# A recurrent cross-attention block feeding an act_gcu block: another order for the first pair of batches, and three moves in the later pairs

## The chip, the cores and the metric

The kernel runs on one core of one Trainium2 chip. A core has TensorE (PE, matmuls; its weight loads are shown as PEld), VectorE (DVE), ScalarE (ACT), GpSimd (POOL), and SyncE (SP), which here only issues DMAs. Each engine works through its own queue in order and waits on semaphores. The metric is the device time of one execution in microseconds (us). Before the change the median of three runs is 735.45 us (733.81 to 736.73).

## The reference

Eight batches, eight heads, 512 tokens and 32 states of width 64 each, in float32; the two weights of the second block come as float64.

```python
scores = scale * x @ state^T;  a = softmax(scores)      # 512 x 32 per head
xread  = a @ state
scores2 = scale * state @ x^T; a2 = softmax(scores2)    # 32 x 512 per head
sread  = a2 @ x
x = concat([xread, sread], axis=2) as (B*544, 512)      # 4352 tokens
h = x @ w_in                                            # 512 -> 2048
g = h * cos(h)
out = g @ w_out                                         # 2048 -> 512
```

## The kernel before, in words

**Layers.** For each batch b the 512 token rows go through 16 tiles f of 128 columns of d_ff ("tile" below is one such f). The attention matrix is not multiplied by the states first: `products` (line 452) multiplies the states with a 512-column part nt of w_in, `products_kept` (457) copies the result into `sw`, and `hidden` (483) multiplies `sw` by the attention matrix `aT` into a PSUM bank h. Then g = h cos(h) in four steps: `gate` (560, ACT, rounds h), `gate2` (567, DVE, the difference), `gate3` (570, ACT, sine), `gate4` (574, DVE, the product into `g_all`). `gate4` is the last reader of h, so a later tile that uses the same bank waits for it. After the eight batches the 256 state rows go through a layer of 16 tiles of their own, the states' layer, and through `state_products`.

**Pairs.** Two batches form a pair. The product with w_out is done for a pair by a Strassen-Winograd scheme: 7 products (class `Product`, 719) of 7 stages each (`ORDER`, 664). A stage (`multiply`, 761) is 8 matmuls of 256 columns in the trace. `follow` (778) is what the other engines do behind a stage: behind stage 1 ACT copies the lower half of the bank and its upper half away, and stage 2 adds into that lower half, so it can only start behind the copies. The sums of columns and rows that the scheme needs are `outer_sum` (1066, DVE or POOL) and `Product.sums` (738, POOL); `halves`, `sw_sums` and `seven_part` (502, 516, 532) do `hidden` for batches 2 to 7 in the same manner, with 7 part products for two tiles. `gate` to `gate4` then work on a pair of tiles, 1024 columns at a time.

**The first pair** (batches 0 and 1, steps 0 to 31) also has to load the float64 weights and make float32 of them. `convert` (213) takes one load of 1 MB in five instructions: ACT "1" and "2" (the magnitude, the low word), DVE "b" (shift left by 3) and "c" (take over the sign, exclusive or), POOL "d" (add the low part). There are 4 half loads (512 columns) and 14 whole ones (1024 columns). For the 14 the shift "b" writes to the two side banks of PSUM (`h_pairs[1]`), and "c" reads it there.
The order of the first pair is not written out. `first_pair_tasks` (1125) lists tasks with an engine, a cost, what they read and write, and a due time in steps; `link` (1524) finds their dependences; `first_pair` (1560) is a planner that puts them on the five queues one by one. It takes the engine that can start soonest; among the tasks of that engine that can start within `NEAR` of the soonest it takes the one due first. A task marked `shares` is a DVE instruction that the planner counts as sharing its memory port with POOL: before the change neither starts while the other's (`lock`) lasts. Where PE would idle long before its first product, it gets filling matmuls (`warm`, 951).

**The later pairs** (from step 32 on) have an order written out by hand: `later_pair` (1638) issues one step. In an even step ACT does `gate` and DVE `gate2`, in an odd step ACT does `gate3` and DVE `gate4`; `go(n)` issues the attention's pieces of list n that `plan` (973) put at this step; `stages` (1099) issues the step's stages of `Product`, one or two. At the end of a step the main loop issues `outer_sum` for that step. In the states' layer `hidden(coming)` issues 8 matmuls for the tile two steps ahead.

Of the kernel before, what the change touches and what calls it, by code (L numbers as in the profile page):

```python
# [11 lines left out]
I32 = mybir.dt.int32  # L12
# [10 lines left out]
def kernel(  # L23
# [189 lines left out]
    def convert(i, p):  # L213
# [8 lines left out]
        shifted = bits if i < 4 else h_pairs[1].bitcast(I32)  # L222
# [6 lines left out]
        elif p == "b":  # L229
            nc.vector.tensor_scalar(shifted, bits, 3, None,  # L230
                                    op0=ALU.logical_shift_left)
        elif p == "c":
            nc.vector.scalar_tensor_tensor(out=bits, in0=raw[:, :, :, 1],  # L233
                                           scalar=-2 ** 31, in1=shifted,
                                           op0=ALU.bitwise_and,
                                           op1=ALU.bitwise_xor)
        else:
            nc.gpsimd.tensor_tensor(bits, bits, e, op=ALU.add)  # L238
# [10 lines left out]
    class Attention:  # L249
# [207 lines left out]
        def products_kept(self, nt, bank=None, c0=0, c1=WC, copy=None,  # L457
                          js=(0, 1)):
            to = at if bank is None else side_banks
            if (self.b, nt) not in sw_of:  # L460
# [258 lines left out]
    class Product:  # L719
# [4 lines left out]
        def __init__(self, name, pr, row):  # L724
# [6 lines left out]
            self.t1 = self.t2 = self.t3 = None  # L731
# [242 lines left out]
    def plan(b):  # L974
        pe, x_act, y_act, x_dve, y_dve, z_act = [
            {s: [] for s in range(NF)} for _ in range(6)]

        def prod(s, b, nt, *bank):
            pe[s].append((b, "products", nt) + bank)
            x_act[s].append((b, "products_kept", nt) + bank)  # L980
# [36 lines left out]
        return pe, x_act, y_act, x_dve, y_dve, z_act  # L1017
# [107 lines left out]
    def first_pair_tasks():  # L1125
# [35 lines left out]
        def conversion(i, due):  # L1161
# [4 lines left out]
            x, narrow = (w, True) if i < 4 else ("sd00 sd01 sd10 sd11", False)  # L1166
            b_cost = n * .0007 + .03 if narrow else dve(n)
            for p, engine, cost, r, wr, sh in (
                    ("1", "act", act(n) + .05, raw, w, False),
                    ("2", "act", act(n) + .05, raw, e, False),  # L1170
                    ("b", "dve", b_cost, w, x, narrow),
                    ("c", "dve", dve(n), raw + " " + x, w, narrow),
# [4 lines left out]
        def attention(b, k):  # L1177
# [30 lines left out]
            m2 = k + 6 if b == 0 else k + 1.0  # L1208
            if b == 0:
                for j in range(2):  # L1210
                    add("dve", .62, lambda j=j: a.sums1((j,)), f"z{z}{j}",
                        f"m1{j}", k + 5)
                add("dve", .46, a.inverse1, "m10 m11", "m10 m11", k + 5,
                    True)
# [9 lines left out]
            if b == 0:  # L1224
                add("act", .2, a.exp2_bias, "m20 m21", "m20 m21", m2)
                for j in range(2):
                    add("act", .72, lambda j=j: a.exp2((j,)),
                        f"at{j} m2{j}", f"xT{2 + j} i2{j} T", m2)
                add("dve", .3, a.inverse2, "i20 i21", "i20 i21", m2 + 2,
                    True)  # L1230
            else:
                add("act", 5.0, a.exps, "at0 at1 m20 m21",
                    f"z{z}0 z{z}1 xT2 xT3 i20 i21 m20 m21", m2)
                for j in range(2):
# [3 lines left out]
                    "m10 m11 i20 i21", k + 7, True)  # L1238
# [54 lines left out]
        def tile_(t, k):  # L1293
# [11 lines left out]
                k + 1.5)  # L1305
# [97 lines left out]
        def p5_tasks(k):  # L1403
# [3 lines left out]
            for i, (r, w) in enumerate(((lo, q1), (hi + " " + q1, q1),  # L1407
                                        (lo + " " + hi, q3)), 1):
                add("pool", 2 * pool(512), lambda i=i: pd.sums(i), r, w,
# [3 lines left out]
            for i in range(5):  # L1413
# [12 lines left out]
                elif i == 2:  # L1426
                    add("dve", .36, follow, "acc0 sums1", "sums2", at_)
                    add("pool", 2 * pool(512), lambda: pd.sums(4),
# [6 lines left out]
        def p3_sums(k):  # L1435
            pd = products_[1]
            add("pool", 2 * pool(512), lambda: pd.sums(1),
# [17 lines left out]
        for step, what in (  # L1455
                (1, lambda: attention_late(0, 7.5)),
                (3, lambda: products(0, 1, 2)),
                (3, lambda: add("pe", .4, lambda: states(1, side_banks[0]),
                                "held0", "sd00 sd01", 7.0)),
                (3, lambda: add("act", .53,  # L1460
                                lambda: states_kept(1, side_banks[0]),
                                "sd00 sd01", "stT1", 10.0)),
                (5, lambda: attention(1, 3)),
                (7, lambda: products(0, 2, 8.5)),
                (11, lambda: products(0, 3, 19.5)),
                (13, lambda: products(1, 0, 21.5)),
                (13, lambda: attention_late(1, 10.0)),
                (13, lambda: inner(0, a11, 5, temps[0], names(TEMPS), 13.0)),
                (15, lambda: sends(2, a22, 8, 17)),
                (15, lambda: sums_of(SQ, A21, A22, add_, 16, "pool")),  # L1470
                (16, lambda: products(1, 1, 16.5)),
                (16, lambda: inner(3, matrix(SQ), SQ, temps[1], E, 16.5)),
                (17, lambda: sums_of(A22, SQ, A11, sub_, 26.5, "pool")),
                (17, lambda: attention(2, 23.5)),
                (18, lambda: sums_of(A21, A11, A21, sub_, 20.0, "dve")),
                (20, lambda: products(1, 2, 14.5)),
                (20, lambda: inner(5, matrix(A21), A21, temps[0],
                                   names(TEMPS), 25.5)),
                (20, lambda: sends(1, a12, 6, 22)),
                (21, lambda: inner(4, matrix(A22), A22, temps[1], E, 28.5)),  # L1480
                (23, lambda: sums_of(SQ, A12, A22, sub_, 32.0, "dve")),
                (24, lambda: inner(6, matrix(SQ), SQ, temps[0], names(TEMPS),
                                   25)),
                (24, lambda: products(1, 3, 27.5)),
# [269 lines left out]
```

## Time and profile before

| what | value |
|---|---|
| three runs | 733.81, 735.45, 736.73 us |
| the profiled execution | 736.73 us, of which the span from first to last instruction is 734.9 us |
| PE busy | 709.1 us (96%) |
| DVE, ACT, POOL busy | 501.4 (68%), 347.0 (47%), 535.5 (73%) |
| 0 to 40 us: PE, DVE, ACT, POOL busy | 32.67, 26.74, 24.03, 15.17 us |
| 40 to 102 us, of 62 | 57.32, 58.55, 56.85, 40.81 us |
| 102 to 158 us, of 56 | 55.49, 45.83, 34.43, 45.31 us |
| 158 to 616 us, of 458 | 450.88, 317.73, 212.86, 365.44 us |
| 616 to 734.9 us, of 118.9 | 112.69, 52.59, 18.84, 68.82 us |

The page gives averages over stages with different limits, so the table cuts the span: the first pair lasts to about 158 us, the later pairs to about 616 us, and the rest is the states' layer and the end. In the trace a float32 matmul appears as two; a tile of the first pair (`hidden`, line 489) is 4 matmuls of 512 columns, 1.72 us at full clock, start to start. A row "x4" of the timeline merges four instructions; PE's records run over into the next by some 0.2 us, so lengths are best read from start to start.

### The profile page before, as it was taken

To read this page: it belongs to the slowest core of one execution; us is meant where nothing else is said; L and a number is where in the kernel's file an instruction comes from. 1 tells how busy PE (TensorE), PEld (TensorE's weight loads), DVE (VectorE), ACT (ScalarE), POOL (GpSimd) and SP (SyncE) were. 2 spreads that over 40 slices of the span, in tenths; PEclk is the share of its full clock that TensorE was granted. 3 is DMA by queue.
4 is the path that set the end of the run, shared out by engine and by line. 5 is a ranking of instruction groups with operands and counts; after the bars stand their busy time and mean duration, and the time that the engine had idled before them with its cause. 6 is when DMAs were issued, how large, how long until landed. Compare 5 with 4: busy or idle time off the path is not lost.

```text
span 734.9 us, 10754 instructions
## 1 busy us (share of the span) xinstructions
PE 709.1 (96%) x3628; PEld 519.4 (71%) x3628; DVE 501.4 (68%) x703; ACT 347.0 (47%) x586; POOL 535.5 (73%) x524
## 2 busy tenths in 40 slices
PE   8798899999999999999999999999999999999997
PEld 4343344467778788786778787877778788888886
DVE  4889979868767567849756687768665367355551
ACT  4699975644544455443634373444634533211110
POOL 1557599557998896579989665879989665799600
PEclk9799999999999999999999999999999999999999
DMA  9787598736346954682248635763235465346652
GB/s 296 255 229 246 177 280 264 174 103 141 86 136 140 217 141 127 133 197 79 81 96 162 159 87 116 157 145 87 72 75 129 112 211 133 103 157 206 162 146 46
DMA packets 204021, 111.33 MB, mean 151 GB/s; under 512 B 149888, under 2 KB 166784, under 8 KB 203968
## 3 DMA queue, kind: packets, MB, share of 16 engines
q1 hardware_dynamic: 202880, 110.14, 57.6%
q8 instruction: 29, 0.48, 0.3%
q10 hardware_dynamic: 960, 0.39, 0.2%
q14 instruction: 24, 0.20, 0.1%
q0 software_dynamic: 128, 0.13, 0.1%
HBM read 87.03 MB, written 23.59 MB: 151 GB/s over the span
## 4 chain that ended last, share of the span: by engine, by line
PE 64%; POOL 21%; DVE 7%; issue 3%; DMA 3%; ACT 2%; SPq 0%; ACTq 0%; DVEq 0%; POOLq 0%
PE o L774 29%; POOL g_all L716 16%; PE h L544 13%; PE h L489 10%; POOL swS_all L522 3%; PE at L313 3%; PE o L641 3%; PE at L879 2%; PE at L418 2%; POOL sw_all L522 2%; DMA g_all<-in_moe_w_in_dram 1%; DMA g_all<-blocks_kept 1%; DVE h L230 1%; PE o L879 1%; DVE w_in L233 1%
## 5 line engine op out<-in xcount | busy, mean ns | idle before, releaser
L716 POOL TENSOR_TENSOR g_all<-g_all 128x512 f32<-128x512 f32 x252 | 333.1, 1352 | 63.9 <-DVE g_all L716 40.8
L774 PE MATMUL o<-g_all 128*128 128x256 f32 x1456 | 344.1, 381 | 2.9 <-POOL g_all L716 2.4
L774 PEld LDWEIGHTS o<-g_all 128*128 128x128 f32 x1456 | 273.6, 190 | 50.8 <-issue 5.0
L565 ACT ACTIVATE q_all<-h 128x1024 int32<-128x1024 f32 (+1 forms) x88 | 73.3, 833 | 86.8 <-PE h L544 37.8
L568 DVE TENSOR_TENSOR q_all<-q_all,h 128x1024 f32<-128x1024 int32 (+1 forms) x88 | 85.2, 969 | 40.2 <-ACT q_all L565 40.0
L585 DVE TENSOR_TENSOR g_all<-h,q_all 128x1024 f32<-128x1024 f32 (+1 forms) x88 | 85.6, 973 | 23.6 <-ACT q_all L571 22.7
L571 ACT ACTIVATE q_all<-q_all,halfpi 128x1024 f32<-128x1024 f32 (+1 forms) x88 | 84.0, 956 | 33.6 <-DVE q_all L568 33.3
L552 DVE TENSOR_TENSOR h<-h,sums_all 128x256 f32<-128x256 f32 x96 | 41.2, 429 | 76.6 <-PE h L544 59.4
L489 PE MATMUL h<-aT_all,sw_all 128*128 128x512 f32 x128 | 63.7, 627 | 4.8 <-DVE g_all L585 4.3
L544 PE MATMUL h<-aS_all,swS_all 128*128 128x256 f32 x192 | 60.3, 396 | 3.1 <-ACT sums_all L530 2.3
L544 PE MATMUL h<-aT_all,sw_all 128*128 128x256 f32 x192 | 59.6, 392 | 3.8 <-DVE g_all L585 3.4
L716 DVE TENSOR_TENSOR g_all<-g_all 128x1024 f32<-128x1024 f32 x42 | 59.9, 1440 | 0.1
L544 PE MATMUL h<-aS_all,sw_all 128*128 128x256 f32 x192 | 58.0, 384 | 0.1
L544 PEld LDWEIGHTS h<-aS_all,swS_all 128*128 128x128 f32 x192 | 33.8, 189 | 27.8 <-issue 12.1
L522 POOL TENSOR_TENSOR swS_all<-sw_all 128x128 f32<-128x128 f32 x48 | 22.5, 468 | 37.9 <-ACT sw_all L463 37.9
L782 ACT COPY o<-o 128x256 f32<-128x256 f32 x26 | 9.3, 357 | 84.8 <-PE o L774 84.8
L489 PEld LDWEIGHTS h<-aT_all,sw_all 128*128 128x128 f32 x128 | 23.4, 197 | 36.7 <-issue 19.8
L544 PEld LDWEIGHTS h<-aT_all,sw_all 128*128 128x128 f32 x192 | 34.5, 189 | 16.3 <-DVE g_all L585 12.1
L789 ACT COPY o<-sums_all 128x256 f32<-128x256 f32 x26 | 9.8, 378 | 70.6 <-PE o L774 70.6
L238 POOL TENSOR_TENSOR w_in<-w_in,aS_all 128x1024 int32<-128x1024 int32 (+1 forms) x10 | 19.6, 1961 | 32.0 <-DVE w_in L233 31.9
L544 PEld LDWEIGHTS h<-aS_all,sw_all 128*128 128x128 f32 x192 | 35.6, 190 | 7.9 <-DVE h L552 2.7
L608 DVE SCALAR_TENSOR_TENSOR held<-o,held 128x512 f32<-128x512 f32 x38 | 25.8, 680 | 13.7 <-PE o L774 13.1
(118 smaller groups left out, 924.6 us busy)
## 6 DMA issues: line engine op xcount, KB each, us to landing
g_all<-blocks_kept SPq DMA_DIRECT2D x206, 256.0 KB, 2.9
blocks_kept<-g_all SPq DMA_DIRECT2D x48, 256.0 KB, 3.6
g_all<-in_moe_w_out_dram SPq DMA_DIRECT2D x8, 1024.0 KB, 5.9
out_dram<-ot SPq DMA_DIRECT2D x128, 64.0 KB, 2.0
g_all<-in_moe_w_in_dram SPq DMA_DIRECT2D x6, 1024.0 KB, 8.0
x_b<-in_x_dram SPq DMA_DIRECT2D x24, 256.0 KB, 4.8
xT<-in_x_dram SPq DMA_DIRECT2D x80, 64.0 KB, 2.9
x_b<-in_x_dram SPq DMA_DIRECT2D x16, 128.0 KB, 3.9
```

Source lines behind the costliest of these rows:

```text
L489: nc.tensor.matmul(out=t.hp, lhsT=t.lhs(i), rhs=t.rhs(i), start=(i == 0), stop=(i == t.kn - 1))
L522: nc.gpsimd.tensor_tensor(o, x1, x2, op=op)
L544: nc.tensor.matmul(out=out_, lhsT=w, rhs=r, start=start, stop=True, skip_group_check=True)
L552: nc.vector.tensor_tensor(o, h2[:, LO], sums_all[:, 0], op=ALU.add)
L565: nc.scalar.activation(t.q.bitcast(I32), t.hp, func=ACTF.Copy, bias=0.25)
L568: nc.vector.tensor_tensor(t.q, t.q.bitcast(I32), t.hp, op=ALU.subtract)
L571: nc.scalar.activation(t.q, t.q, func=ACTF.Sin, bias=halfpi, scale=-TWO_PI)
L585: nc.vector.tensor_tensor(g, t.hp, t.q, op=ALU.mult)
L608: nc.vector.scalar_tensor_tensor(out=out.t[:, ch], in0=bank, scalar=TWO_PI, in1=b.t[:, ch], op0=ALU.mult, op1=ALU.add)
L716: engine.tensor_tensor(o[:, i:i + n], x1[:, i:i + n], x2[:, i:i + n], op=ALU.subtract)
L774: nc.tensor.matmul(out=o, lhsT=ring[(self.first + k) % NB][:, i], rhs=g[:, i], start=(start and i == 0), stop=(i == QT - 1), skip_group_ch ...
L879: nc.tensor.matmul(out=x, lhsT=b(i), rhs=end_weights[w][:, :, i // QT, i % QT], start=(start and i == 0), stop=(i == NH - 1), skip_group_c ...
```

## The change

1. **Conversion.** The shift "b" of all loads goes back into the weights' own place in SBUF, and "c" reads it there. The side banks are no longer held by a conversion, and all "b" and "c" are marked `shares`.
2. **The planner.** The lock goes one way: a `shares` task that would start while POOL's latest task runs is moved behind it, and POOL itself is not held up by DVE. The two `inverse` steps are no longer marked. `Product.sums` on POOL is costed at `4 * pool(512)` in place of 2. All due times, the due times of the conversions (`CONV_DUE`), `PACE` and `NEAR` are others. What the tasks do is the same, but for one filling matmul group less (13 in place of 14 in PE's order).
3. **Later pairs, copies.** Where state products are issued in an odd step, ACT's copies of them go from that step to the next even one, behind `gate`, the first of the seven part products and `gate2`.
4. **Later pairs, outer sums.** DVE's outer sums that use row 3 and stand at the end of an even step go into the following odd step, behind its `gate4`.
5. **States' layer.** Where a step has stages 1 and 2 of a product, stage 1 goes ahead of `hidden(coming)`, which then stands between the two stages.

```diff
@@ convert
-        shifted = bits if i < 4 else h_pairs[1].bitcast(I32)
...
-            nc.vector.tensor_scalar(shifted, bits, 3, None,
+            nc.vector.tensor_scalar(bits, bits, 3, None,
                                     op0=ALU.logical_shift_left)
...
-                                           scalar=-2 ** 31, in1=shifted,
+                                           scalar=-2 ** 31, in1=bits,
@@ plan
-        pe, x_act, y_act, x_dve, y_dve, z_act = [
-            {s: [] for s in range(NF)} for _ in range(6)]
+        pe, x_act, y_act, x_dve, y_dve, z_act, w_act = [
+            {s: [] for s in range(NF)} for _ in range(7)]
...
-            x_act[s].append((b, "products_kept", nt) + bank)
+            (w_act[s + 1] if s % 2 else x_act[s]).append(
+                (b, "products_kept", nt) + bank)
@@ conversion
-            x, narrow = (w, True) if i < 4 else ("sd00 sd01 sd10 sd11", False)
-            b_cost = n * .0007 + .03 if narrow else dve(n)
...
-                    ("b", "dve", b_cost, w, x, narrow),
-                    ("c", "dve", dve(n), raw + " " + x, w, narrow),
+                    ("b", "dve", n * .0007 + .03, w, w, True),
+                    ("c", "dve", dve(n), raw + " " + w, w, True),
@@ first_pair_tasks: due times, for instance
-                (1, lambda: attention_late(0, 7.5)),
-                (3, lambda: products(0, 1, 2)),
+                (1, lambda: attention_late(0, 1)),
+                (3, lambda: products(0, 1, 3)),
...
-                (11, lambda: products(0, 3, 19.5)),
-                (13, lambda: products(1, 0, 21.5)),
+                (11, lambda: products(0, 3, 11)),
+                (13, lambda: products(1, 0, 15)),
...
-                first(step - 4, step - 0.5)
+                first(step - 4, step + 1)
...
-                    second(i, step + 10.0)
+                    second(i, step + 2)
...
-    CONV_DUE = (1.9, 1.9, 3.0, 5.1, 5.3, 5.4, 9.4, 10.5, 10.6, 11.7, 12.2, 13.3, 13.0, 15.2)
-    PACE, NEAR, SEND = 3.6, 0.1, 2.5
+    CONV_DUE = (3, 4.5, 3.5, 6, 7.5, 7, 9, 9.5, 10.5, 11, 12, 14.5, 14, 15)
+    PACE, NEAR, SEND = 3.8, 0.3, 2.5
@@ first_pair
-                    asked = max(free[e], ready[t])
-                    shares = t.shares or e == "pool"
-                    starts[t] = max(asked, lock) if shares else asked
+                    at_ = max(free[e], ready[t])
+                    if t.shares and pool_busy[0] <= at_ < pool_busy[1]:
+                        at_ = pool_busy[1]
+                    starts[t] = at_
...
-            if t.shares or t.engine == "pool":
-                lock = end
+            if t.engine == "pool":
+                pool_busy = at_, end
@@ later_pair
         elif coming is not None:
+            if [k for _, k in stage_at[step][0:2]] == [1, 2]:
+                stages(step, 1)
             hidden(coming)
         if even or not t.paired:
             gate2(t)
+        go(6)
...
             gate4(t.mate)
+            while sums_late:
+                outer_sum(*sums_late.pop(0))
@@ main loop
         for what in outer_at[step]:
-            outer_sum(*what)
+            if even and what[0] is dve and 3 in what[2:5]:
+                sums_late.append(what)
+            else:
+                outer_sum(*what)
```

## The prediction

> **What bounds the kernel now.** I read the busy shares first, then PE's waits, then the timeline where they lie. PE is busy 709.1 of 734.9 us, so a gain must be an idle stretch of PE or a slower clock, and any engine that makes PE wait is a loss. PE's waits (us in total, times, longest):
>
> ```profile
> PE h L489 <- DVE g_all L585: 4.3, 3, 2.6
> PE at L401 <- ACT xT L362: 4.2, 1, 4.2
> PE h L544 <- DVE g_all L585: 3.4, 8, 0.4
> PE o L774 <- POOL g_all L716: 2.4, 3, 0.8
> ```
>
> The first two lie in the first pair, the last two later. PE's timeline at the start (start, length):
>
> ```profile
> 21.14 0.64 PE L313 MATMUL h<-w_in,st_all 64*32 64x256 f32 x8
> 26.02 1.97 PE L401 MATMUL at<-ident,xT 128*128 128x128 f32 x8 [4.24 <-ACT xT L362]
> 29.55 6.15 PE L489 MATMUL h<-aT_all,sw_all 128*128 128x512 f32 x8 [0.53 <-ACT sw_all L463]
> 40.46 1.98 PE L489 MATMUL h<-aT_all,sw_all 128*128 128x512 f32 x4
> ```
>
> PE stands still from 21.4 to 26.0 us; then the granted clock is 0.71 (20 to 30 us) and 0.77 (30 to 40), and tiles 0 and 1 take 6.15 us where two tiles take 3.44 later. Tile 2 starts at 40.46. From 40 to 102 us DVE is busy for 58.55 of 62: up to there the first pair is bound by DVE's queue, from then to 158 us by PE (55.49 of 56).
>
> **Part 1, the conversion.** The shift "b" by place, from the line's own view:
>
> ```profile
> L230 DVE TENSOR_SCALAR h<-w_in x6: 1207/1228/1229, 29.8 to 61.6; 128x1024 int32<-128x1024 int32 x6
> L230 DVE TENSOR_SCALAR w_in<-w_in x4: 405/420/426, 15.3 to 17.1; 128x512 int32<-128x512 int32 x4
> ```
>
> A whole shift into PSUM costs 1.2 us start to start. In SBUF half a load takes 0.42, and 0.34 start to start (16.43, 16.78, 17.11), so a whole one lies between 0.34 and 0.67; I take 0.65, near twice the half. 14 x 0.55 = 7.7 us less work for DVE. The exclusive or "c" stays at 1.2 (with all operands in SBUF and POOL idle, an outer sum of the same size took 1.18 to 1.22). What speaks against it is in DVE's and POOL's timelines:
>
> ```profile
> 17.45 1.28 DVE L233 SCALAR_TENSOR_TENSOR w_in<-g_all,w_in 128x512 int32<-128x512 int32 x2
> 19.87 1.77 DVE L233 SCALAR_TENSOR_TENSOR w_in<-g_all,w_in 128x512 int32<-128x512 int32 x1
> 33.59 1.22 DVE L233 SCALAR_TENSOR_TENSOR w_in<-g_all,h 128x1024 int32<-128x1024 int32 x1
> ```
> ```profile
> 18.29 2.80 POOL L238 TENSOR_TENSOR w_in<-w_in,aS_all 128x512 int32<-128x512 int32 x2 [14.43 <-DVE w_in L233]
> 32.44 4.90 POOL L238 TENSOR_TENSOR w_in<-w_in,aS_all 128x1024 int32<-128x1024 int32 x2 [7.55 <-DVE w_in L233]
> ```
>
> The one at 19.87 reads SBUF alone, found POOL in an instruction that ended at 21.09, and ended 0.6 behind it: 1.77 in place of 0.68. The one at 33.59 reads PSUM, with POOL busy, and took its 1.22. So the change opens 28 instructions (14 shifts, 14 exclusive ors) to POOL's, which last up to 2.37 us. The wait w for each: DVE's 12 sums and normalisations in SBUF alone between 90 and 158 us exceed their undisturbed time by 0.40 on average, those behind 158 us by about 0.2; an unguarded start in the middle of a 2.37 us instruction, with POOL busy 60% of the time, would be 0.7. I take 0.33, since the planner still moves DVE out of the way, and keep 0.2 to 0.7.
>
> The Trainium skill bears on this twice over. GPSIMD Engine Reference, Key points, says that POOL shares its SBUF interfaces with DVE and contends with DVE instructions that have two SBUF inputs or run in a 2-port mode; the 19.87 row agrees for two inputs, no row shows the shift against POOL. By that rule all 28 are exposed, by the row alone the 14 exclusive ors: 28 x 0.33 = 9.2 us or 4.6 us.
>
> **Part 2, the order of the first pair.** I walked DVE's new queue with the durations above. It shifts only two half loads, and brings the sums, the inverse and the normalisation of batch 0 ahead of the maxima and of the other two half loads. The sums end at 19.4; the inverse waits for POOL's second addition (20.4); two spreads and two normalisations of 0.62 end at 23.3. Tiles 0 and 1 can start there, not at 29.55, behind a pause of PE of about 1.9 us. At full clock they end at 26.8; at half clock, which costs 2.7 more, at 29.5. I take full: the 2.71 us pause at 63.2 us was followed by a clock of 1.00. `gate4` of tile 0 then stands behind two whole shifts, two copies and two exclusive ors, and ends at 34.2 (40.2 before), so that tile 2 starts at 34.4. DVE has 22.0 us of work up to there, so its queue runs 12.2 us behind its work; before, 40.2 - 24.8 = 15.4.
>
> On the clock, TensorE: Matmul & The Clock Gate, Part 1, states a half clock behind an idle window of some 3.4 us. By it too the new pause keeps the clock; were it wrong, 2.7 us would come on top.
>
> The order's rows, each by its duration (0.62 for 512 columns, 1.2 for 1024), give DVE's work up to `gate4` of a tile, before and after: tile 5, 50.1 and 35.3; tile 10, 64.6 and 58.0; tile 16, 83.6 and 75.9; tile 31, 124.1 and 117.2. Before, `gate4` ended at 66.0, 81.8, 101.7 and 156.5. So the start is much earlier, but the conversions put off come between tiles 5 and 16. There the queue bounds. At tile 16: 75.9 work + 12.2 + 28 x 0.33 of waits + pauses. Pauses were 18.1 - 15.4 = 2.7 before; I take 4, since ACT's queue is as full (79.3 of work up to tile 16, before 78.8). Sum 101.3, before 101.7: nothing won, nothing lost, to 0.4 us. PE's work issued ahead of tiles 16 to 18 differs by -0.8 to +1.3 us, one filling matmul group (0.86) counted: nothing. Behind tile 16 PE bounds in both, and before loses only 0.9 us around each of the small products; I take the same. POOL has the room (45 of 56 us). SP's fetches keep their number and nearly their order; where one comes later, the conversion behind it does, and that is inside the sums. **First pair: 0**, ends -5.3 (w 0.2, pauses 2.7: 96.4) and +10 (w 0.7: 111.7). PE had over 10 us of pauses and half clock to give before 64 us, so the lower end is open.
>
> **Part 3, the copies.** The two copies (1.07) per batch, six batches, leave ACT at 179.27 and stand behind `gate` (1.04) and the two copies of `seven_copies` (0.75). `gate` starts 0.9 earlier, but its reader `gate2` waits for DVE until 182.09 anyway. The copies end near 182.2; the next scores write the same banks on PE, at 182.25 before and about 0.3 earlier by part 4, so they can wait 0.25, with all of PE behind them. Five batches have scores there: between 0 and +1.3; I take **+0.7**. POOL's column sums, which read the copies, start at 184.92: covered.
>
> **Part 4, the outer sums.** DVE around a pair of tiles, and who waits:
>
> ```profile
> 175.53 2.08 DVE L716 TENSOR_TENSOR g_all<-g_all 128x1024 f32<-128x1024 f32 x1
> 178.20 1.21 DVE L585 TENSOR_TENSOR g_all<-h,q_all 128x1024 f32<-128x1024 f32 x1
> 186.06 1.46 DVE L716 TENSOR_TENSOR g_all<-g_all 128x1024 f32<-128x1024 f32 x1
> 188.38 1.21 DVE L585 TENSOR_TENSOR g_all<-h,q_all 128x1024 f32<-128x1024 f32 x1
> 189.64 0.70 PE L544 MATMUL h<-aT_all,sw_all 128*128 128x256 f32 x2 [0.42 <-DVE g_all L585]
> ```
>
> The sums at 175.53 and 186.06 are the two that move behind `gate4` (L585). PE's starts around these two `gate4` stretch by 0.27 and 0.58; the same at 337 and 347, 495 and 505 us. The first goes. At the second, the sums pile up: three in a row behind 178, so `gate2` comes 1.6 later (183.7), and `gate4` is freed less; I take half of it. 3 x (0.27 + 0.3) = **-1.7**, ends 0 (the pile costs what it frees) and -2.6. POOL's sums that read them have a step to spare.
>
> **Part 5, the states' layer.**
>
> ```profile
> 619.04 1.89 PE L774 MATMUL o<-g_all 128*128 128x256 f32 x8
> 620.96 0.36 ACT L782 COPY o<-o 128x256 f32<-128x256 f32 x1 [2.43 <-PE o L774]
> 621.23 0.38 ACT L783 COPY sums_all<-o 128x256 f32<-128x256 f32 x1
> 621.71 1.97 PE L774 MATMUL o<-g_all 128*128 128x256 f32 x8 [0.78 <-POOL g_all L716]
> ```
>
> Stage 1 starts at 619.04, lasts 8 x 0.216 = 1.73, and stage 2 starts 0.95 later. POOL is named, but ACT's two copies end just ahead of it. The same 0.95 stands at 658 and 678 us. PE's new order has `hidden` (1.73 us) between these stages in just these three places, and the copies need 0.75: 3 x 0.95 = **-2.9**. If POOL really is late, nothing goes: 0.
>
> **Sum.** 0 + 0.7 - 1.7 - 2.9 = -3.9 us. The profiled execution took 736.73 us (span 734.9 and 1.8 around it): 732.8. It lies 1.28 above the median, so the forecast is 731.5. A difference under 0.5% (3.7 us) can hardly be told from none.
>
> **Rivals.**
> *The port decides, slower.* w at 0.7 makes the first pair 10 us longer; less 3.9, 741.5. From w = 0.48 on the change is a loss (75.9 + 12.2 + 4 + 28w = 101.7 + 3.9). For it: POOL busy 40.8 of 62 us, instructions of 2.37 us. Against: the planner dodges, and POOL too waited at times (one took 3405 ns, not 2373).
> *The early start is kept, faster.* w at 0.2 and pauses as before: -5.3 - 3.9, 726.2. For it: DVE has 14.8 us less to do up to tile 5. Against: ACT's queue has nothing less by tile 16.
> *The moves don't do what they say.* Parts 3 to 5 cancel and the gaps turn up elsewhere: 735.4. For it: the named releaser in part 5, the pile in part 4.
>
> **Numbers.** My forecast 0.38 (its own range 728 to 735), slower rival 0.27, faster rival 0.23, no effect 0.12. The range from 725 to 742 takes in w from 0.2 to 0.7 and leaves out less than 2 in 10. Faster by over 0.5% (under 731.8): the faster rival and half of mine, 0.42. Slower (over 739.1): most of its rival, 0.26; the rest 0.32.
>
> **What would show it.** Right: tile 2 at 34 to 36 us and a clock of 1.00 by 30; `gate4` of tile 16 ending at 98 to 105; the first stage product near 140; no 0.95 between the three stage pairs. Wrong: whole shifts in SBUF over 1 us on average, POOL's additions over 3 us, PE waiting for L584 between tiles 9 and 16 by more than 5 us, or PE waiting for copies ahead of the scores.

## The result, and the profile after

The changed kernel takes 743.02 us (median of 5 runs, 741.52 to 743.44), the kernel before 735.45 (733.81 to 736.73): a ratio of 1.0098, 95% interval 1.0078 to 1.0117. It is slower by 1%, where the forecast was 0.5% faster; 743.02 also lies outside the range of 725 to 742. The profiled execution took 743.28 us, its span is 741.5, so 6.6 us longer than before's 734.9.

Two marks that stand in both orders of PE cut this difference: the last matmul of the first `products` behind the first pair, and the last matmul of all `products` (states times w_in; the expectations below call the second mark "the last scores"). Before, they start at 163.11 and 594.55 us; after, at 167.83 and 598.71. So in these two executions the first pair costs 4.7 us, the later pairs give back 0.6, and the rest, from the second mark through the states' layer to the end, takes 142.8 in place of 140.3 us.

The early start came as walked. PE's timeline of the changed kernel (start, length; in brackets the idle time ahead and what ended it):

```profile
23.19 3.67 PE L488 MATMUL h<-aT_all,sw_all 128*128 128x512 f32 x8 [0.74 <-DVE aT_all L393]
34.05 3.70 PE L488 MATMUL h<-aT_all,sw_all 128*128 128x512 f32 x8 [1.33 <-DVE g_all L584]
...
73.71 1.98 PE L488 MATMUL h<-aT_all,sw_all 128*128 128x512 f32 x4 [2.05 <-DVE g_all L584]
78.55 1.99 PE L488 MATMUL h<-aT_all,sw_all 128*128 128x512 f32 x4 [0.97 <-DVE g_all L584]
82.56 3.06 PE L488 MATMUL h<-aT_all,sw_all 128*128 128x512 f32 x4 [2.02 <-DVE g_all L584]
87.68 1.98 PE L488 MATMUL h<-aT_all,sw_all 128*128 128x512 f32 x4 [0.49 <-DVE g_all L584]
97.09 3.61 PE L488 MATMUL h<-aT_all,sw_all 128*128 128x512 f32 x4 [3.47 <-DVE g_all L584]
```

Tiles 0 and 1 take 3.67 us at full clock from 23.19 (29.55 before, 6.15 long), and tile 2 starts at 34.05 (forecast 34.4, before 40.46). Tile 8 still leads by 11.2 us (58.5 against 69.7). Then PE waits for `gate4` (L584) again and again, and with tile 17 it is 5.7 us behind before (104.1 against 98.4). The last wait brings the clock down too: the granted clock is 0.62 from 96 to 100 us, and tile 16, at 97.09, takes 3.45 us, start to start, in place of 1.72. PE's waits between 68 and 100 us, of the kernel before and of the changed one (us in total, times, longest):

```profile
PE h L489 <- DVE g_all L585: 1.8, 2, 1.3
```
```profile
PE h L488 <- DVE g_all L584: 9.0, 5, 3.5
```

VectorE's timeline where the lead is lost shows why `gate4` is late:

```profile
80.14 1.76 DVE L229 TENSOR_SCALAR g_all<-g_all 128x1024 int32<-128x1024 int32 x1
...
83.02 3.40 DVE L232 SCALAR_TENSOR_TENSOR g_all<-g_all 128x1024 int32<-128x1024 int32 x1
...
88.14 1.65 DVE L393 TENSOR_TENSOR aT_all<-aT_all,xT 128x512 f32<-128x512 f32 x1
...
98.47 1.75 DVE L229 TENSOR_SCALAR g_all<-g_all 128x1024 int32<-128x1024 int32 x1
100.25 2.18 DVE L232 SCALAR_TENSOR_TENSOR g_all<-g_all 128x1024 int32<-128x1024 int32 x1
```
```profile
79.03 4.01 POOL L1326 TENSOR_TENSOR g_all<-g_all 128x512 f32<-128x512 f32 x2
82.99 2.34 POOL L237 TENSOR_TENSOR g_all<-g_all,aS_all 128x1024 int32<-128x1024 int32 x1
```

L229 is the shift, L232 the exclusive or, L393 a normalisation, L237 and L1326 are POOL's addition and its sums. The shift is 0.68 long where nothing is in its way, the exclusive or 1.21, the normalisation 0.65. The exclusive or of 83.02 ended at 86.42, which is 1.1 us, about its own length, behind the end of POOL's work at 85.33.

The last stretch has a single loss. The three gaps of 0.95 between stage pairs are gone, which is 2.85 us; in their place PE stands still once, behind the matmul that starts at 690.3. All three engines of the changed kernel there:

```profile
688.81 1.89 PE L772 MATMUL o<-g_all 128*128 128x256 f32 x8
694.27 3.65 PE L772 MATMUL o<-g_all 128*128 128x256 f32 x8 [3.58 <-issue]
```
```profile
682.17 0.42 DVE L783 TENSOR_TENSOR sums_all<-o,sums_all 128x256 f32<-128x256 f32 x1 [5.87 <-PE o L772]
682.52 10.11 DVE L849 TENSOR_TENSOR g_all<-g_all 128x128 f32<-128x128 f32 x8
692.55 0.68 DVE L567 TENSOR_TENSOR q_all<-q_all,h 128x512 f32<-128x512 int32 x1
...
693.78 0.40 DVE L789 TENSOR_TENSOR o<-o,sums_all 128x256 f32<-128x256 f32 x1
```
```profile
680.97 9.86 POOL L715 TENSOR_TENSOR g_all<-g_all 128x512 f32<-128x512 f32 x8
695.50 1.26 POOL L824 TENSOR_TENSOR held<-held 128x512 f32<-128x512 f32 x1 [4.67 <-ACT q_all L564]
```

L849 are the eight state sums (`state_sums`, differences of columns that the states' layer needs for its own product). One of them is long, the other seven take 0.28 each; this is the line's own view (shortest, median, longest in ns):

```profile
L849 DVE TENSOR_TENSOR g_all<-g_all x8: 281/284/8456, 682.5 to 692.3; 128x128 f32<-128x128 f32 x8
```

The long one, the first, ended at 690.98, and POOL's eight sums ended at 690.83. L789, whose bank PE's next stage needs, came behind it all and ended at 694.18, just ahead of PE's 694.27. Counted from the end of the matmul ahead, start to start, PE's pause is 3.74 us (the row's 3.58 counts from the end of the record). The slower clock that follows (0.79 on average from 692 to 700 us) adds to it.

### The profile page after: what moved, and what is told of

The parts are those of the page before. It is cut to its first block, busy times and chain, and to the rows that moved or that the text cites. A ratio compares the mean times of both kernels' runs of the same rounds, so it can differ in the third digit from the quotient of the medians.

```text
span 741.5 us, 10731 instructions
## 1 busy us (share of the span) xinstructions
PE 709.5 (96%) x3626; PEld 523.0 (71%) x3626; DVE 508.7 (69%) x703; ACT 347.7 (47%) x586; POOL 539.8 (73%) x524
## 4 chain that ended last, share of the span: by engine, by line
PE 56%; POOL 25%; DVE 9%; issue 4%; DMA 3%; ACT 2%; SPq 1%; POOLq 0%; DVEq 0%; ACTq 0%
PE o L772 27%; POOL g_all L715 19%; PE h L543 13%; PE h L488 6%; POOL swS_all L521 4%; PE at L312 3%; PE at L877 2%; PE o L640 2%; DMA held<-in_state_dram 2%; DVE g_all L715 1%; PE at L417 1%; DVE q_all L567 1%; DVE g_all L232 1%; DVE g_all L584 1%; PE o L877 1%
## 5 line engine op out<-in xcount | busy, mean ns | idle before, releaser
L584 DVE TENSOR_TENSOR g_all<-h,q_all 128x1024 f32<-128x1024 f32 (+1 forms) x88 | 85.6, 972 | 27.0 <-ACT q_all L570 26.1
L551 DVE TENSOR_TENSOR h<-h,sums_all 128x256 f32<-128x256 f32 x96 | 41.3, 430 | 81.9 <-PE h L543 64.6
L543 PE MATMUL h<-aS_all,sw_all 128*128 128x256 f32 x192 | 58.1, 384 | 3.6 <-DVE h L551 3.5
L543 PE MATMUL h<-aS_all,swS_all 128*128 128x256 f32 x192 | 60.2, 395 | 0.8 <-POOL swS_all L521 0.8
L543 PE MATMUL h<-aT_all,sw_all 128*128 128x256 f32 x192 | 58.7, 387 | 2.2 <-DVE g_all L584 2.1
L521 POOL TENSOR_TENSOR swS_all<-sw_all 128x128 f32<-128x128 f32 x48 | 25.4, 530 | 45.4 <-ACT sw_all L462 45.4
L543 PEld LDWEIGHTS h<-aS_all,swS_all 128*128 128x128 f32 x192 | 34.0, 189 | 24.8 <-issue 13.1
L543 PEld LDWEIGHTS h<-aS_all,sw_all 128*128 128x128 f32 x192 | 35.6, 190 | 12.3 <-issue 4.1
L237 POOL TENSOR_TENSOR w_in<-w_in,aS_all 128x1024 int32<-128x1024 int32 (+1 forms) x10 | 22.3, 2243 | 29.7 <-DVE w_in L232 25.4
L543 PEld LDWEIGHTS h<-aT_all,sw_all 128*128 128x128 f32 x192 | 35.2, 190 | 11.9 <-DVE g_all L584 7.3
L462 ACT COPY sw_all<-at 128x512 f32<-128x512 f32 x48 | 25.8, 591 | 18.5 <-PE at L312 18.3
```

What stands on the lines that cost most here:

```text
L462: (copy or nc.scalar.copy)(sw_of[self.b, nt][:, j, c0:c1], to[j][:, c0:c1])
L521: nc.gpsimd.tensor_tensor(o, x1, x2, op=op)
L543: nc.tensor.matmul(out=out_, lhsT=w, rhs=r, start=start, stop=True, skip_group_check=True)
L551: nc.vector.tensor_tensor(o, h2[:, LO], sums_all[:, 0], op=ALU.add)
L584: nc.vector.tensor_tensor(g, t.hp, t.q, op=ALU.mult)
```

## The experiments

All ratios stand against runs of the kernel before on the same chip. "To the first mark" and "from the last mark" below are the two marks of the section above. To the first it takes 160.9 to 163.6 us in the profiles of the seven kernels whose first pair is before's to the instruction, so single executions differ by 2.7 us there; with the changed first pair it takes 165.8 to 167.8 in three profiles.

**The first pair alone** (parts 1 and 2; the other three undone):

```diff
-            (w_act[s + 1] if s % 2 else x_act[s]).append(
+            x_act[s].append(
-            if [k for _, k in stage_at[step][0:2]] == [1, 2]:
-                stages(step, 1)
-            if even and what[0] is dve and 3 in what[2:5]:
+            if False:
```

> The changed kernel with all its edits behind the first pair undone (the copies, the outer sums, the states' layer go back to where they were). Theory A: of the 6.6 us by which the changed kernel's profiled span is longer, the first pair is 4.7 (its products end at 167.37 in place of 162.66), the rest lies behind; so this kernel is 735.4 + 4.7 = 740.1 us, with the products' stage at 690 us without a pause. Rival B (the first pair's delay is made up later, because the later pairs have slack, and the loss is made at the end): 735.4 to 736.5. Rival C (the later edits lose nothing by themselves and only a late first pair brings the pause at 690 us about): 743, with the pause at 690 us still there.

739.77 us, ratio 1.0061 (1.0049 to 1.0073): theory A. From the last mark to the end it takes 140.3 us, as before, without a pause near 690 us.

**The later edits alone** (parts 3 to 5 on the kernel before):

> The kernel before with the three edits of the later pairs and of the states' layer alone; its first pair is untouched. Theory A: -0.5 for the copies and the outer sums together, -2.85 for the three gaps of 0.95 and +5.5 for the pause and the half clock near 690 us: 735.4 + 2.15 = 737.6 us, with the pause of 3.7 us there. Rival B (the pause comes from the later edits meeting a first pair that ends 4.7 late): no pause, 735.4 - 3.35 = 732.0. Rival C (the outer sums behind the gate cost more than seen): over 739.

739.04 us, 1.0049 (1.0037 to 1.0061), 1.4 above theory A and at the edge of rival C. Between the marks it takes 430.9 us, though, no more than other kernels (430.3 to 431.7), so the outer sums don't show the loss that rival C puts on them there. The pause is there (3.77 us at 683.5), so the late first pair has no part in it; 144.1 us from the last mark.

**The states' layer alone** (part 5 on the kernel before):

```diff
         elif coming is not None:
+            if [k for _, k in stage_at[step][0:2]] == [1, 2]:
+                stages(step, 1)
             hidden(coming)
```

> The kernel before with one edit: in an odd step whose next stages are 1 and 2, both are issued ahead of the hidden layer. Theory A: the pause at 690 us is made by this edit alone, because the second stage's subtraction on VectorE (it waits for PE until 682.2 in the changed kernel) now stands ahead of the eight state sums, which then meet GpSimd's eight sums; so -2.85 + 5.5: 735.4 + 2.65 = 738.1 us. Rival B (the pause needs the moved copies or the late outer sums): 735.4 - 2.85 = 732.6, no pause. Rival C (even the gaps of 0.95 don't go without the others): 735.4.

The edit moves stage 1 alone ahead of `hidden`, not both stages, as the expectation says; but stage 2 comes earlier by it too, ahead of the state sums, where before it stood behind them. 738.85 us, 1.0049 (1.0034 to 1.0065): the pause is there, so it is this edit's. That is 0.75 over theory A's number, and says nothing yet of its reason.

**The same with stage 2 at the end of its step**, so that VectorE has the state sums ahead of stage 2's subtraction again:

```diff
+        behind = False
...
         elif coming is not None:
             if [k for _, k in stage_at[step][0:2]] == [1, 2]:
                 stages(step, 1)
+                behind = True
             hidden(coming)
...
-        if even:
+        if even and not behind:
             stages(step, 1)
...
-        if not even:
+        if not even and not behind:
             stages(step, 1)
```

> The kernel before with stage 1 between the two stages as in the change, but stage 2 left at the end of the step, behind the state sums: PE's order is that of the change, VectorE's has the eight state sums ahead of the second stage's subtraction, as before. Theory A (VectorE's order makes the pause): the three gaps of 0.95 go and no pause comes, 735.4 - 2.85 = 732.6 us. Rival B (PE's order itself makes the pause, as the stage's buffer comes free later): a pause of some 3.7 us at 690 us remains, 738. Rival C (the gaps only move): 735.4.

741.19 us, 1.0080 (1.0067 to 1.0094). Theory A fell: the pause did not go, it grew to 6.4 us, which rival B, PE's order, would also allow. VectorE's and POOL's timelines of this kernel:

```profile
671.22 14.95 DVE L851 TENSOR_TENSOR g_all<-g_all 128x128 f32<-128x128 f32 x8
686.09 0.42 DVE L785 TENSOR_TENSOR sums_all<-o,sums_all 128x256 f32<-128x256 f32 x1
```
```profile
674.54 9.82 POOL L716 TENSOR_TENSOR g_all<-g_all 128x512 f32<-128x512 f32 x8
```

The first state sum took 13.29 us and ended at 684.51; POOL, without a break since long before 671, ended at 684.36. So the order on VectorE is not the cause. The first state sum, which came while POOL worked from one instruction straight into the next, was served only when POOL stopped. In the kernel before, POOL did stop:

```profile
674.06 2.49 POOL L826 TENSOR_TENSOR held<-held 128x512 f32<-128x512 f32 x2
677.51 10.01 POOL L716 TENSOR_TENSOR g_all<-g_all 128x512 f32<-128x512 f32 x8 [0.95 <-PE o L774]
```

It waited 0.95 us for PE, whose stages stand later by the gaps ahead of it that part 5 takes away; in the kernels with part 5 this stop is gone. The first state sum, begun at 674.22, was let in there, after 2.48 us (L851 below). But not every VectorE instruction of two SBUF operands waits for such a stop. In the same run of POOL, which began at 637.28, outer sums (L716, 1.18 alone) ended while POOL went on, behind the one instruction that they met. VectorE and POOL of the kernel before:

```profile
648.23 1.68 DVE L716 TENSOR_TENSOR g_all<-g_all 128x1024 f32<-128x1024 f32 x1
...
674.22 7.25 DVE L851 TENSOR_TENSOR g_all<-g_all 128x128 f32<-128x128 f32 x8
```
```profile
L851 DVE TENSOR_TENSOR g_all<-g_all x8: 282/772/2478, 674.2 to 680.1; 128x128 f32<-128x128 f32 x8
```
```profile
637.28 36.83 POOL L716 TENSOR_TENSOR g_all<-g_all 128x512 f32<-128x512 f32 x26 [4.78 <-DVE g_all L716]
```

**The states' layer, and state sums one pair of tiles later** (the first eight go to the second pair of tiles, the second eight to the third):

```diff
+    put_off = []
...
-            state_sums(t.mate)
-            state_sums(t)
+            put_off.append(t)
+            for u in put_off[:-1] if t.f < 4 else put_off[:]:
+                put_off.remove(u)
+                state_sums(u.mate)
+                state_sums(u)
```

> The kernel before with the states' layer edit of the change, and the first eight state sums put off by one pair of tiles (the third pair makes its own and the second's, so that the last pair has only its own). The theory of VectorE's order fell: with the state sums first, one of them stood for 13.29 us, and with the subtraction first for 8.49 us, each time until GpSimd's unbroken run of 1.27 us sums ended (684.36, 686.44). Theory A now: a state sum that meets GpSimd in a run waits for the end of the whole run; the 0.95 us gaps of PE that the edit takes away had broken that run (GpSimd idle for 0.95 at 676.56 before, and the state sum that waited there took 2.48). Put off to about 687.4, the eight sums meet GpSimd between two runs: the pause of PE goes, 735.3 - 2.85 = 732.4 us. Rival B (PE's order makes the pause, by the bank that comes free later): the pause of 3.7 remains, 738.8. Rival C (they only wait elsewhere, in the next run, and delay the products' ends): 734 to 737, without the gaps of 0.95.

732.46 us, 0.9967 (0.9954 to 0.9981): theory A, to 0.1 us, and faster than the kernel before. PE's order is that of the two kernels above, so rival B falls. The first eight sums take 2.98 us at 685.55, beside a POOL that has just ended its run (timelines of this kernel, VectorE and POOL), and PE has no pause:

```profile
685.55 2.98 DVE L852 TENSOR_TENSOR g_all<-g_all 128x128 f32<-128x128 f32 x8
```
```profile
675.21 9.87 POOL L716 TENSOR_TENSOR g_all<-g_all 128x512 f32<-128x512 f32 x8
685.77 1.27 POOL L826 TENSOR_TENSOR held<-held 128x512 f32<-128x512 f32 x1 [0.70 <-DVE held L608]
```

From the last mark it takes 137.6 us, 2.8 less than before: the three gaps.

**The changed kernel with the same put-off**, all its edits kept:

> The changed kernel, all its edits kept, with the first eight state sums put off by one pair of tiles as in the kernel that takes 732.5 us. Theory A (the whole loss of the last stretch is one state sum that stood behind GpSimd's run for 8.46 us): from the last scores to the end 137.6 us in place of 142.8, so 743.0 - 5.2 = 737.8 us, and the pause of 3.74 at 690 us is gone. Rival B (the later first pair shifts the two engines against each other, so that the put-off sums meet another run): 740 to 743. Rival C (the moved copies and outer sums bring their own wait near the end): 739 to 740.

737.47 us, 1.0023 (1.0011 to 1.0036): theory A, 0.3 under its number. The last stretch is 137.6 us. So the whole loss behind the last mark was that one state sum.

**The outer sums alone** (part 4 on the kernel before):

> The kernel before with the outer sums of the last row behind the gate of the odd step, and nothing else. Theory A (read from the changed kernel: the gaps of 0.27 and one of 0.58 per stretch of 158 us go, but the product that is behind an outer sum waits 0.7 to 0.8 twice in a stretch): 735.3 - 2.6 + 4 = 735 to 737. Rival B (the waits of 0.7 come from the moved copies, not from the sums): 735.3 - 1.7 = 733.6. Rival C (nothing measurable): 735.3.

737.64 us, 1.0033 (1.0015 to 1.0050), 0.6 over theory A's range, and not as theory A had it. Between the marks it takes 430.3 us, before 431.4 and the kernels without part 4 430.6 to 431.3: the sums gain at most about 0.4 to 1 there. The loss is in the last stretch, 144.8 us, though this edit touches nothing in it: POOL's stop ahead of its eight sums, 0.95 us in before, is 0.17 here, and the state sums catch it worse (VectorE and POOL of this kernel):

```profile
670.90 12.33 DVE L851 TENSOR_TENSOR g_all<-g_all 128x128 f32<-128x128 f32 x8
```
```profile
674.19 10.18 POOL L716 TENSOR_TENSOR g_all<-g_all 128x512 f32<-128x512 f32 x8 [0.17 <-PE o L774]
```

Here they went in turns: seven of the eight took 1.24 to 1.40 us, one POOL instruction each.

**The copies alone** (part 3 on the kernel before):

> The kernel before with the state products' two copies behind the copies of the seven products, and nothing else. Theory A (read from the changed kernel: the next scores wait 0.24 to 0.35 for them, five times): 735.4 + 1.4 = 736.8 us at most, 736 as predicted. Rival B (the copies are hidden): 735.4. Rival C (they change the rhythm in the last stretch so that a state sum meets GpSimd in an unbroken run, as happened with the outer sums alone: 144.9 us from the last scores to the end in place of 140.4): 738 to 740 with a pause of PE near 680 us.

737.12 us, 1.0009 (0.9990 to 1.0029): not to be told from no change, so A and B stay open. PE's starts in the scores stretch by 0.35 at 259.3 us, and there is no pause near 680, which speaks against C.

**The shift in SBUF with before's due times, the planner told so** (part 1, planned anew):

```diff
-        shifted = bits if i < 4 else h_pairs[1].bitcast(I32)
+        shifted = bits
...
-            x, narrow = (w, True) if i < 4 else ("sd00 sd01 sd10 sd11", False)
+            x, narrow = w, True
```

> The kernel before with the conversion's shift in SBUF for all loads, and the planner told so; its due times, its lock between VectorE and GpSimd, and the later pairs are before's. It takes 14 whole shifts from 1.2 to 0.65 us, 7.7 us less work, and opens 28 instructions to GpSimd. Theory A (the waits of the conversion eat what it saves; in the changed kernel 28 x 0.30 = 8.5 us): within 1 us of before, 734.4 to 736.4. Rival B (it is the conversion that makes the first pair late): 739 to 740, as with the first pair's edits together. Rival C (before's order keeps VectorE out of GpSimd's way, and only the new order doesn't): 735.3 - 4 = 731.

747.93 us, 1.0174 (1.0153 to 1.0195): none of the three. The first mark comes at 174.4. It is not the instruction alone: the planner, whose lock now guards 28 more tasks, made another order.

**The shift in SBUF in before's order to the instruction** (only the first line above):

> The kernel before with the conversion's shift in SBUF and with nothing else: the planner is not told, so that every engine's order is before's to the instruction (the shift in SBUF with the planner told so made another order, and 747.9 us). Theory A (the first pair's term as the prediction had it: 7.7 us less work for VectorE, 28 x 0.30 = 8.5 us of waits on GpSimd): 735.4 + 0.8 = 736.2 us, between 734.5 and 738. Rival B (in an order made for PSUM, the exposed instructions meet GpSimd's unbroken runs and wait for their ends): over 740. Rival C (the place is a gain by itself, and the 747.9 came from the order that the planner made of it): 728 to 732.

740.13 us, 1.0053 (1.0036 to 1.0069): rival B. The lines' own views in this kernel:

```profile
L230 DVE TENSOR_SCALAR g_all<-g_all x8: 679/682/2530, 33.5 to 99.7; 128x1024 int32<-128x1024 int32 x8
L233 DVE SCALAR_TENSOR_TENSOR g_all<-g_all x8: 1218/1568/2802, 36.1 to 101.1; 128x1024 int32<-128x1024 int32 x8
```

The 14 whole shifts add up to 13.92 us (17.11 before), the 14 exclusive ors to 25.71 (17.01 before). The shift alone is 0.68 in place of 1.22; 13 us of waiting (0.47 for each of the 28) takes more than that back.

**The new order with the shift in PSUM, planned anew** (part 2 alone):

> The changed kernel's planner, due times and order of the first pair, but the shift of the later loads into PSUM's side banks as before; the later pairs are before's. Theory A (order and conversion each cost: 7.7 us more work and 8.5 us less waiting nearly cancel): within 1.5 us of the first pair's edits together, 738.3 to 741.3. Rival B (the conversion makes the first pair late, the order keeps its early start): tile 8 leads by 11 us and a good part of it lasts, 728 to 732. Rival C (neither alone costs, only both together): 735.3.

740.35 us, 1.0067 (1.0047 to 1.0086): theory A's number. The early start is there (`gate4` of tile 0 ends at 36.6), but not its lead (tile 16 at 108.1). As the planner made a third order here, the run doesn't tell what the shift's place is worth.

**The changed kernel's order to the instruction, with the shift in PSUM:**

> The order of the changed kernel's first pair to the instruction, with the shift of the later loads written to PSUM's side banks again; the planner is not told, the later pairs are before's. Against the first pair's edits together (739.8 us) it has 14 x 0.55 = 7.7 us more work on VectorE and its 28 conversion instructions no longer wait for GpSimd (8.5 us of waits in the changed kernel). Theory A (the two cancel, the order itself is what costs 4 to 5): 738.5 to 740.5. Rival B (the waits on GpSimd are what the new order loses, and they cost more than their sum as PE's pauses bring the half clock): 733 to 736. Rival C (the side banks are held by products in this order, and the shift waits for PE): over 743.

744.99 us, 1.0125 (1.0096 to 1.0154). This is rival C's number, but the run tells little: in this order products still stand in the side banks when a shift is written there, so that the output is wrong, and PE has waits for conversions that neither kernel has (2.3 us for L230, 1.7 for L233).

**Without POOL's additions.** Two kernels leave out the 14 whole additions of the conversion (and with them the low part of the float64 weights), the kernel before and the first pair alone:

```diff
-        else:
+        elif i < 4:
             nc.gpsimd.tensor_tensor(bits, bits, e, op=ALU.add)
```

> The kernel before with GpSimd's additions of the conversion left out for the 14 whole loads (the low part of each 64-bit number is then not added, so the output differs in the last bits; every other instruction and the order of all engines stay). It takes some 34 us of work from GpSimd in the first pair; VectorE's conversion reads PSUM here and did not wait for it. Theory A (VectorE's queue bounds this stretch, and its exposed instructions waited some 5 us in all up to 105 us; loads also are ready 2.4 us earlier): 730 to 734. Rival B (the additions lay on the way of the loads to PE): under 728.

> The first pair's edits together (739.8 us), with the same 14 additions of GpSimd left out. VectorE's instructions stand 17.2 us longer than the shortest of their kind up to 105 us there, 5.1 in the kernel before beside the price of its shifts into PSUM; without the additions most of both should go. Theory A (what the new order and the shift in SBUF lose is the waiting for GpSimd): it is then as fast as the kernel before with the same left out, or up to 7 us faster, -7 to 0 between the two, where they stood 4.5 apart the other way. Rival B (the order itself puts PE's work late, whatever GpSimd does): it stays 3 to 5 us slower than the kernel before with the same left out.

735.25 us, 1.0002 (0.9984 to 1.0020), and 731.22 us, 0.9946 (0.9926 to 0.9965). The kernel before doesn't notice that some 34 us of POOL's work are gone, a miss of both theories on it. The new first pair goes from 4.5 us behind before to 4.0 ahead of it. No engine's order differs but for POOL's missing additions. Up to 105 us VectorE's instructions stand some 17 us over the shortest of their kind in the first pair alone, and some 7 without the additions; PE waited only 0.4 us for additions themselves, in both. What the new first pair loses is therefore its waiting for POOL, on VectorE. Its shifts are undisturbed now:

```profile
L229 DVE TENSOR_SCALAR g_all<-g_all x8: 680/686/691, 36.1 to 90.7; 128x1024 int32<-128x1024 int32 x8
```

## Why the prediction was wrong

**Part 1, right in its parts.** A whole shift in SBUF is 0.68 long where undisturbed, 0.60 start to start (0.65 taken). Waits were taken as 0.33 for each of the 28 instructions; in the changed kernel the 14 shifts exceed their shortest by 5.3 us and the 14 exclusive ors by 3.4, 0.31 for each of the 28. Before had no row of a shift against POOL; the changed kernel has them, and shifts wait as exclusive ors do. Of the two counts that the prediction weighed, 28 by the Trainium skill (GPSIMD Engine Reference, Key points) and 14 by the row of before, these rows agree with the skill's. The sign of error named in advance, whole shifts over 1 us on average, came: 14.82 / 14 = 1.06.

**Part 2, the walk of the start, right;** tile 2 and the clock of 1.00 came as said. PE's idle time ahead of tile 0 was 0.74 us and not about 1.9, as filling matmuls stand in it, so the price of such a pause was not put to the test.

**Part 2, the sum at tile 16, too small: this is the failed step "nothing won, nothing lost, to 0.4 us".** It set `gate4` of tile 16 at 101.3: 75.9 work, 12.2 and 4 of idle time, 9.2 of waits. It ended at 105.2, with VectorE busy for 88.69 and idle for 16.5:

```profile
0.00:105.20 105.20, 89.31 (x403) 39.02 (x404) 88.69 (x117) 80.49 (x122) 62.89 (x39) 0.95 0.81 244
```

(The columns are PE, its weight loads, VectorE, ScalarE, GpSimd, then clock and DMA.) The idle time was right (16.2); the busy time is 3.6 us more than 75.9 + 9.2. The sum had waits for the 28 conversion instructions alone. Those that it left out, of the changed kernel and of before:

```profile
L373 DVE TENSOR_SCALAR i_all<-i_all x3: 1151/1246/2031, 19.6 to 70.7; 128x32 f32<-128x32 f32 x1, 128x2 f32<-128x2 f32 x1, 128x34 f32<-128x34 f32 x1
L393 DVE TENSOR_TENSOR aT_all<-aT_all,xT x4: 651/680/1653, 22.4 to 88.1; 128x512 f32<-128x512 f32 x4
```
```profile
L374 DVE TENSOR_SCALAR i_all<-i_all x3: 161/177/805, 24.1 to 79.9; 128x32 f32<-128x32 f32 x1, 128x2 f32<-128x2 f32 x1, 128x34 f32<-128x34 f32 x1
```

Three tiny inverse steps took 4.43 us in place of 1.14, and one normalisation 1.65 in place of 0.68. These inverses are steps that the change no longer marks for the planner (all three of the first pair, and two `halves` steps, not only the two named in the description of the change); the prediction priced the wait of one of them. So `gate4` of tile 16 ends 3.5 us later than before. PE, with its last pause and the half clock at tile 16, is 5.7 behind at tile 17 and 4.7 at the mark; what it makes up between was not followed. PE's 9.0 us of waits for L584 is the other sign named in advance (over 5).

The rival "the port decides" had the right mechanism and the right sign, and put it into w alone: it asked for w over 0.48, and w was 0.31. The runs without POOL's additions show its size: 8.5 us between 4.5 behind and 4.0 ahead.

**Part 3, +0.7:** the waits ahead of the scores came, 0.24 to 0.35 at five places; alone +0.1% at an interval that holds no change. **Part 4, -1.7:** too good. Between the marks parts 3 and 4 together give 0.6 against this one execution of before and nothing against the other kernels with before's later pairs. The gap of 0.27 went; the seven part products (L543) then waited for L551 (`seven_sum`) instead, behind the piled-up sums ("PE h L543 <- DVE h L551: 3.5, 6, 0.7" in the list of PE's waits). That the pile costs what it frees was this part's end at 0.

**Part 5, -2.9, the second failed step.** The gaps went, 2.85 us, and the copies were their reason as argued. What the step left out is who else used them: POOL's stop at 676.55 hung on PE's gaps, and it was the place where VectorE's first state sum got in. With a POOL that doesn't stop, the sum stood 8.46 us and made a pause of 3.74 with a slower clock behind it, +5.3 (142.8 - 140.3 + 2.85; the put-off took 5.2 of it back). This state sum stands in the trace of before at 2.48 us in place of 0.28, and the prediction didn't ask what ended it.

Sum by the measured terms: 4.7 - 0.6 - 2.85 + 5.3 = 6.6 us, which is the difference of the spans, as the marks cut it into these parts; each term is read from single executions.

## What to carry to other kernels

Before moving work on VectorE or taking an idle gap from PE, list every VectorE instruction on SBUF alone that falls into a stretch where GpSimd works without a break, the tiny ones too. Here most waited for the one GpSimd instruction that they met, but one sum of 0.28 us stood for the whole run. An idle gap is not only lost time; see which queue draws breath in it. Here the gap of 0.95 us was worth removing only together with moving the first eight small sums out of GpSimd's run: then the time went from 735.4 to 732.5 us, and without it to 738.9.

## What the runs showed of the hardware

- A VectorE instruction of two SBUF operands can stand till the end of an unbroken run of GpSimd, not for one instruction: the first state sum took 8.46 us (GpSimd ended 0.15 us before it did), 8.49, and 13.29 us, for 0.28 of work. It did so in all fourteen kernels where it met such a run. Others did not: the outer sum of 648.23 took 1.68 in place of 1.18 and ended inside the very run that held the state sum in the kernel before, and state sums that were already being served when GpSimd began its run went in turns with its instructions, 1.24 to 1.40 us each. What decides between the two was not tried.
- The shift of 32-bit integers in SBUF, with one operand, waits as well (up to 2.55 us for 0.68 of work, in before's order), and so does a one-operand step on 128x34 elements (2.03 us in the changed kernel, 0.18 before). The shift with PSUM as output did not: 1202 to 1229 ns in all fourteen of the kernel before, eleven of them beside a GpSimd at work.
- Taking 34 us of GpSimd's work out of the stretch that VectorE bounds changed nothing where VectorE's conversions write and read PSUM (ratio 1.0002), and moved the time by 8.5 us in the changed first pair, where they stay in SBUF and the order is another.
